# RWKV attention and two MoE stages on one core: converted weight words written over their raw tile, the converter's scratch in PSUM for two instructions longer, and another place for the rounding of the last block

## The chip, the cores and the metric

The kernel runs on one core of one Trainium2 chip. The metric is the device time of the whole program in microseconds. TensorE (PE) multiplies, with its weight loads shown apart (PEld); VectorE is DVE, ScalarE is ACT, GpSimd is POOL, and SyncE (SP) issues the transfers.

## The reference

Three stages follow one another. Only matrix products and elementwise steps over 3072 tokens matter here.

```python
# attention: 4 batches, 8 heads, 768 steps, head size 48
cur = einsum('bhd,bhe->bhde', u * k_t, v_t)
y_t = einsum('bhd,bhde->bhe', r_t, state + cur)
state = w_t[..., None] * state + einsum('bhd,bhe->bhde', k_t, v_t)
x = y.transpose(0, 2, 1, 3).reshape(3072, 384)
# first MoE: w_in (384 x 2048), w_out (2048 x 384)
h = x @ w_in
x = (h - tanh(h)) @ w_out
# second MoE: w_in2 (384 x 1024), w_out2 (1024 x 384)
h = x @ w_in2
solu = h * softmax(h)
ln = (solu - mean) / sqrt(var + 1e-6) * g_ln
out = ln @ w_out2
```

The weights arrive as 64-bit floats. A product is made of three matmuls on pairs of a rounded value and its remainder ("hi" and "lo"), so every weight and every activation is needed in these two parts.

## The kernel before, in words

**Order of the work.** The tokens are six blocks of 512 (i = 0 to 5). In the first MoE a block takes 16 steps, one for each 128 columns of w_in (m = 0 to 15), so there are 96 steps. `part1` of a step makes hp, nine matmuls into one of two PSUM banks (L334), and from it the activation; `part2` follows two steps later with nine matmuls into the three banks x2p (L357). The attention of 24 chunks of 128 tokens is spread between the steps of blocks 0 to 4, four chunks ahead of the loop. After the steps the second MoE works on 24 token tiles (b_h L412, norm, b_t L446, b_o L457). The code is written in this order, and a scheduler then settles the order of instructions on each engine by an estimate of its own; each engine runs its list in order.

**The activation in `part1`.** ACT squares hp into t (L339), DVE makes y = hp·t (L340), ACT makes the polynomial's other factor p (L342), DVE makes y = (p + c)·y (L344), ACT writes a range check over q (L345) whose only use is a sum for a flag. In block 0 p overwrites hp in PSUM and ACT rounds y into gs[0] (L347); in the other blocks p is written to the tile q in SBUF, where the check then overwrites it, and POOL rounds y (L349). POOL always makes the remainder gs[1] = y − gs[0] (L350). t, q and y have two buffers each, gs three.

**The converter, `convert` (L113 to L131).** It turns a raw tile of 128 x 768 word pairs into float values and splits them. ACT scales the low words in place (L118). For each of two halves of 384, DVE shifts and masks the high words into a scratch `a` (L125) and joins the sign and top bits (L126); the result stands in cv_x, a tile of its own in SBUF with two buffers. One DVE add over all 768 words brings in the low words (L127, shown as an operation on 1536 16-bit halves). ACT scales one half where asked (L129) and makes hi (L130); POOL makes lo (L131). `conv_a` does this for the 16 weight tiles wa of the first MoE, ahead of and during block 0, with `a` in a bank of the three-bank PSUM pool that attention uses (tile cv_a). `conv_b` does it for the eight tiles wb of the second MoE, one every second step from the first step of block 5 on (`LAST`), with `a` in cv_x itself. wb takes the place of buffers that attention frees, so it can't be written before block 5. Raw tiles have two buffers; in blocks 1 to 4 they are loaded again for a check of the weights (`check_pair`, ACT).

Of the kernel before, what the change touches and what calls it, by code (L numbers as in the profile page):

```python
# [8 lines left out]
F32 = mybir.dt.float32  # L9
F32R = mybir.dt.float32r  # L10
U32 = mybir.dt.uint32
# [3 lines left out]
ALU = mybir.AluOpType  # L15
# [4 lines left out]
NT, DM, FF, FF2 = 3072, 384, 2048, 1024  # L20
# [3 lines left out]
BLK = 512  # L24
UB = BLK // C
NB = NT // BLK
# [29 lines left out]
class Kern:  # L56
# [52 lines left out]
    def convert(self, pool, raw, hi, lo, scale=None, bank=None):  # L109

        nc, v = self.nc, self.nc.vector  # L113
        flat = raw.rearrange("p i f two -> p (i f) two")
        H_, L_ = flat[:, :, 1], flat[:, :, 0]
        x = pool.tile([128, 2 * DM], U32, tag="cv_x", name="cv_x")
        xf = x.bitcast(F32)
        nc.scalar.activation(L_, L_, AF.Copy, scale=2.0**-29)  # L118
        for i in range(2):
            s = slice(i * DM, (i + 1) * DM)  # L120
            if bank is None:
                a = x[:, s]
            else:
                a = bank.tile([128, 4, C], F32, tag="a", name="cv_a").rearrange("p j t -> p (j t)")[:, 0:DM].bitcast(U32)
            v.tensor_scalar(a, H_[:, s], 3, 0x3FFFFFF8, ALU.logical_shift_left, ALU.bitwise_and)  # L125
            v.scalar_tensor_tensor(x[:, s], H_[:, s], 0xC0000000, a, ALU.bitwise_and, ALU.bitwise_or)  # L126
        v.tensor_tensor(x, x, L_, ALU.add)  # L127
        if scale is not None:
            nc.scalar.activation(xf[:, DM:], xf[:, DM:], AF.Copy, scale=scale)  # L129
        nc.scalar.copy(hi, xf)  # L130
        nc.gpsimd.tensor_tensor(lo, xf, hi, ALU.subtract)  # L131
# [196 lines left out]
    def part1(self, i, m):  # L328
        nc, v, g = self.nc, self.nc.vector, self.nc.gpsimd
        hp = self.ps_h.tile([128, BLK], F32, tag="h", name="hp")  # L330
        xs = self.xs[i % 2]
        seq = [(a, b, j) for j in range(KM) for a, b in ((1, 0), (0, 1), (0, 0))]
        for n, (a, b, j) in enumerate(seq):
            self.mm(hp, self.wa[:, a, m, j * 128:(j + 1) * 128], xs[:, b, j], start=n == 0, stop=n == len(seq) - 1)  # L334
        t = self.gp.tile([128, BLK], F32, tag="t", name="t")
        q = self.gp.tile([128, BLK], F32, tag="q", name="q")
        y = self.gp.tile([128, BLK], F32, tag="y", name="y")
        gs = self.gs.tile([128, 2, BLK], F32R, tag="g", name="g")
        nc.scalar.activation(t, hp, AF.Square)  # L339
        v.tensor_tensor(y, hp, t, ALU.mult)  # L340
        p = hp if i == 0 else q
        nc.scalar.activation(p, t, AF.Square, bias=self.c_fsb, scale=F_S)  # L342
        col = 2 * NU + i * NM + m
        v.scalar_tensor_tensor(y, p, F_E, y, ALU.add, ALU.mult)  # L344
        self.last_act = nc.scalar.activation(q, t, AF.Relu, bias=self.c_t2, accum_out=self.flags[:, col:col + 1])  # L345
        if i == 0:
            nc.scalar.copy(gs[:, 0], y)  # L347
        else:
            g.tensor_scalar(gs[:, 0], y, 1.0, 1.0, ALU.mult, ALU.mult)  # L349
        g.tensor_tensor(gs[:, 1], y, gs[:, 0], ALU.subtract)  # L350
        return gs
# [121 lines left out]
@with_exitstack  # L473
def rwkv_moe_moe_kernel(ctx: ExitStack, tc: tile.TileContext, *args):
    nc = tc.nc
    K = Kern(tc, args)
    const = ctx.enter_context(tc.tile_pool(name="const", bufs=1))
    dram = ctx.enter_context(tc.tile_pool(name="dram", bufs=1, space=bass.MemoryType.DRAM))
    K.x2d = dram.tile([DM, NT], F32, name="x2d")
    safe = fast_path(tc, K, const)  # L480
    ok = nc.values_load(safe, min_val=0, max_val=1)
    with tc.If(ok < 1):
        general_path(tc, K, const)


def fast_path(tc, K, const):
    nc = tc.nc

    def pool(stack, name, bufs=1, side=None, **kw):
        return stack.enter_context(tc.tile_pool(name=name, bufs=bufs, side=side, reuse_waits="tile", **kw))  # L490

    K.load_act_set()
    K.setup(const)
    K.gl = const.tile([128, NM2], F32, name="gl")
    L, R, R2 = ExitStack(), ExitStack(), ExitStack()
    cv = pool(L, "cv", 2)
    cvr = pool(L, "cvr", 2)
    K.gp = pool(L, "gp", 2)
    K.gs = pool(L, "gs", 3)
    wp = pool(L, "wp")  # L500
    xp1 = pool(L, "xp1")
    xp0 = pool(R, "xp0", side="right")
    att = pool(R, "att", side="right")
    ps_x = pool(L, "ps_x", space=PSUM)
    K.ps_h = pool(L, "ps_h", 2, space=PSUM)
    K.ps_a = pool(R, "ps_a", 3, side="right", space=PSUM)
    K.wa = wp.tile([128, 2, NM, 2 * DM], F32R, name="wa")
    K.x2p = [ps_x.tile([128, BLK], F32, name=f"x2p{d}") for d in range(KM)]
    K.att_setup(att, xp0, xp1)
    K.setup_mask(K.kh[0])  # L510

    raw, gs = {}, {}
    OFF = -18
    LAST = (NB - 1) * NM
    nc.sync.dma_start(out=K.ub, in_=K.u.rearrange("h d -> (h d)").partition_broadcast(128))
    nc.scalar.activation(K.ub, K.ub, AF.Copy, scale=-1.0)
    K.att_load(0)
    K.att_load(1)
    nc.sync.dma_start(out=K.gl, in_=K.g_ln.rearrange("(k p) -> p k", p=128))

    early = 2
    SK = 2.1
    first = [(k + SK * u, K.att_pre if k < 0 else getattr(K, f"att_{k}"), u) for u in range(UB) for k in range(-1, 5)]
    first += [(SK * (u - 2) + 1.05, K.att_load, u) for u in range(2, UB + 2)] + [(SK * UB - 1, K.att_pre, UB)]
    first += [(2.0 * m, lambda m: K.conv_a(cv, cvr, m), m) for m in range(early)]
    for _, f, n in sorted(first, key=lambda e: e[0]):
        f(n)
    for s in range(-2, NB * NM + 2):
        if 0 <= s < NB * NM:
            gs[s] = K.part1(*divmod(s, NM))  # L530
        for k in (4, 0, 1, 2, 3):
            u, rem = divmod(s - OFF - k, 4)
            if rem == 0 and UB <= u < NU:
                getattr(K, f"att_{k}")(u)
        u, rem = divmod(s - OFF + 1, 4)
        if rem == 0 and UB < u < NU:
            K.att_pre(u)
        u, rem = divmod(s - OFF + 6, 4)
        if rem == 0 and UB + 1 < u < NU:
            K.att_load(u)  # L540
        if 0 <= s - 2 < NB * NM:
            K.part2(*divmod(s - 2, NM), gs.pop(s - 2))
        if 0 <= s < NM - early:
            K.conv_a(cv, cvr, s + early)
        if s == LAST:
            R.close()
            wb = pool(R2, "wb", side="right")
            K.bx = pool(R2, "bx", 2, side="right")
            K.wb = wb.tile([128, 2, NM2, 2 * DM], F32R, name="wb")
            ps_r = pool(R2, "ps_r", side="right", space=PSUM)  # L550
        if 0 <= s - LAST < NM and (s - LAST) % 2 == 0:
            K.conv_b(cv, cvr, (s - LAST) // 2)
        n, due = divmod(3 * (s - NM), 7)
        if 0 <= n < NM + NM2 and due < 3:
            K.check_pair(cvr, n)
    safe = K.safe_flag(const)
    L.close()

    K.bp = pool(L, "bp", 2)
    K.bs = pool(L, "bs", 4)  # L560
    ps_l = pool(L, "ps_l", space=PSUM)
    K.ps_t = pool(L, "ps_t", 2, space=PSUM)
    K.ps_b = (ps_r, ps_l)
    hs, ts = {}, {}
    for n in range(NTT + 2):
        if n < NTT:
            hs[n] = K.b_h(K.load_x2(n), n)
        if 0 <= n - 1 < NTT:
            ts[n - 1] = K.b_t(hs[n - 1][0])
        if 0 <= n - 2 < NTT:  # L570
            K.b_o(n - 2, ts.pop(n - 2), hs.pop(n - 2)[1])
    L.close()
    R2.close()
    return safe
# [196 lines left out]
```

## Time and profile before

| what | value |
|---|---|
| median of three runs | 837.1 us (836.93 to 837.52) |
| the profiled execution's own time | 833.47 us |
| its span | 831.7 us |
| PE busy | 779.4 us (94%) |
| DVE busy | 548.6 us (66%) |
| ACT busy | 490.5 us (59%) |
| POOL busy | 377.2 us (45%) |
| mean granted TensorE clock | 0.979 |

The shares are averages over stages that differ. Block 0 runs from about 77 to 177 us of the span, blocks 1 to 4 up to 513, block 5 to 597, and the second MoE from there.

### The profile page before, as it was taken

Reading aid. Unit: us, or ns where it says so; the run is one execution under the profiler, and the core shown is the slowest. Engines: PE = TensorE matmul, PEld = TensorE weight load, DVE = VectorE, ACT = ScalarE, POOL = GpSimd, SP = SyncE. Lnnn points to the kernel's source line nnn. Section 1 sums busy time; section 2 is a strip of 40 time slices with the busy share of each in tenths; the row PEclk is TensorE's granted clock in tenths of the full one; section 3 lists DMA queues with packets and bytes.
Section 4 is the critical chain, followed back from the end, with each engine's and each line's share of the span. In section 5 each row is a group of like instructions: output and inputs, shape, how many; then the busy total and the mean of one; then the engine's idle time right before and its main releaser. Section 6 shows DMA issues by size and latency. Waiting matters only on the chain.

```text
span 831.7 us, 13450 instructions
## 1 busy us (share of the span) xinstructions
PE 779.4 (94%) x4706; PEld 649.1 (78%) x4706; DVE 548.6 (66%) x997; ACT 490.5 (59%) x928; POOL 377.2 (45%) x360
## 2 busy tenths in 40 slices
PE   3778988999999999999999999889989999999996
PEld 2656766778878888888888788667879999999996
DVE  4688889666664566565556763895287577667763
ACT  3436776677666767677677765655445454445442
POOL 3544765655555655556556465676412111111110
PEclk9988998899999999999999999999999999999998
DMA  9966567435455554463434220410021111111101
GB/s 164 166 107 127 138 146 151 136 100 115 90 120 114 125 108 105 107 157 81 119 100 130 82 81 25 140 50 2 10 67 39 48 39 48 39 48 39 48 29 33
DMA packets 151309, 74.32 MB, mean 89 GB/s; under 512 B 107328, under 2 KB 142784, under 8 KB 151232
## 3 DMA queue, kind: packets, MB, share of 16 engines
q1 hardware_dynamic: 151232, 73.37, 37.0%
q8 instruction: 39, 0.64, 0.3%
q14 instruction: 38, 0.31, 0.1%
HBM read 61.54 MB, written 9.44 MB: 85 GB/s over the span
## 4 chain that ended last, share of the span: by engine, by line
PE 75%; DVE 11%; DMA 4%; issue 2%; POOL 2%; ACT 2%; SPq 2%; DVEq 0%; ACTq 0%; POOLq 0%
PE hp L334 19%; PE x2p L357 18%; PE o L457 12%; PE h L412 11%; PE qk L254 3%; PE tp L218 3%; DVE cv_x L126 2%; PE tt L446 2%; DVE cv_x L127 2%; PE y L296 2%; PE y L293 2%; DMA raw<-in_moe_w_out_dram 1%; DVE cv_x L125 1%; DMA raw<-in_moe_w_in_dram 1%; PE kt L260 1%
## 5 line engine op out<-in xcount | busy, mean ns | idle before, releaser
L357 PE MATMUL x2p<-g,wa 128*128 128x512 f32 x864 | 226.4, 401 | 9.0 <-POOL g L350 4.6
L334 PE MATMUL hp<-xs,wa 128*128 128x512 f32 x864 | 225.8, 403 | 6.7 <-POOL wa L131 3.2
L334 PEld LDWEIGHTS hp<-xs,wa 128*128 128x128 f32 x864 | 162.5, 192 | 45.2 <-POOL wa L131 3.7
L357 PEld LDWEIGHTS x2p<-g,wa 128*128 128x128 f32 x864 | 160.3, 191 | 46.0 <-POOL g L350 6.3
L350 POOL TENSOR_TENSOR g<-y,g 128x512 fp32r<-128x512 f32 x96 | 129.3, 1347 | 17.4 <-ACT g L347 9.7
L340 DVE TENSOR_TENSOR y<-hp,t 128x512 f32<-128x512 f32 x96 | 66.2, 689 | 106.6 <-ACT t L339 103.6
L457 PE MATMUL o<-wb,ts 128*128 128x384 f32 x576 | 110.0, 341 | 1.0 <-DVE ts L448 1.0
L345 ACT ACTIVATE q<-t,cst 128x512 f32<-128x512 f32 x96 | 69.5, 724 | 68.1 <-DVE y L344 67.8
L412 PE MATMUL h<-wb,x2s 128*128 128x512 f32 x432 | 103.8, 392 | 2.8 <-DVE so L432 2.4
L349 POOL TENSOR_SCALAR g<-y 128x512 fp32r<-128x512 f32 x80 | 53.9, 674 | 114.8 <-DVE y L344 111.4
L457 PEld LDWEIGHTS o<-wb,ts 128*128 128x128 f32 x576 | 100.5, 188 | 2.9 <-DVE ts L448 1.3
L412 PEld LDWEIGHTS h<-wb,x2s 128*128 128x128 f32 x432 | 80.6, 188 | 19.8 <-issue 3.0
L339 ACT ACTIVATE t<-hp 128x512 f32<-128x512 f32 x96 | 56.6, 591 | 44.8 <-PE hp L334 44.6
L437 POOL TENSOR_TENSOR st<-st,cst 128x1 f32<-128x1 f32 x24 | 13.5, 563 | 136.2 <-DVE st L436 134.8
L344 DVE SCALAR_TENSOR_TENSOR y<-q,y 128x512 f32<-128x512 f32 x80 | 65.4, 818 | 10.6 <-ACT q L342 5.6
L342 ACT ACTIVATE q<-t,cst 128x512 f32<-128x512 f32 x80 | 57.7, 722 | 2.0
L435 ACT ACTIVATE e<-so 128x1024 f32<-128x1024 f32 x24 | 25.4, 1059 | 49.4 <-DVE so L434 49.4
L425 DVE TENSOR_REDUCE st<-h 128x1 f32<-128x1024 f32 x24 | 29.4, 1224 | 28.6 <-PE h L412 27.1
L428 DVE TENSOR_REDUCE part<-e 128x32 f32<-128x1024 f32 x24 | 29.3, 1220 | 27.9 <-ACT e L427 27.9
L218 PE MATMUL tp<-ident,rkw 128*128 128x128 f32 x264 | 41.9, 292 | 6.0 <-DMA rkw<-in_w_dram 5.7
L402 POOL TENSOR_TENSOR x2s<-x2s 128x384 fp32r<-128x384 f32 x24 | 24.4, 1018 | 48.3 <-ACT x2s L401 40.0
L131 POOL TENSOR_TENSOR wa<-cv_x,wa 128x768 fp32r<-128x768 f32 x16 | 29.4, 1838 | 35.3 <-ACT wa L130 35.3
(114 smaller groups left out, 1211.1 us busy)
## 6 DMA issues: line engine op xcount, KB each, us to landing
raw<-in_moe_w_out_dram SPq DMA_DIRECT2D x48, 384.0 KB, 4.0
raw<-in_moe_w_in_dram SPq DMA_DIRECT2D x64, 144.0 KB, 3.2
raw<-in_moe_w_in_dram SPq DMA_DIRECT2D x16, 384.0 KB, 3.1
rkw<-in_w_dram SPq DMA_DIRECT2D x24, 192.0 KB, 4.3
rkw<-in_r_dram SPq DMA_DIRECT2D x24, 192.0 KB, 4.5
rkw<-in_k_dram SPq DMA_DIRECT2D x24, 192.0 KB, 3.9
vt<-in_v_dram SPq DMA_DIRECT2D x24, 192.0 KB, 4.4
x2d<-x2o SPq DMA_DIRECT2D x18, 256.0 KB, 2.2
```

The lines of the kernel that those rows point to most:

```text
L218: self.nc.tensor.transpose(p[:, j], self.rkw[u % 2][:, i, 2 * j:2 * j + 2, :], self.ident)
L334: self.mm(hp, self.wa[:, a, m, j * 128:(j + 1) * 128], xs[:, b, j], start=n == 0, stop=n == len(seq) - 1)
L339: nc.scalar.activation(t, hp, AF.Square)
L340: v.tensor_tensor(y, hp, t, ALU.mult)
L342: nc.scalar.activation(p, t, AF.Square, bias=self.c_fsb, scale=F_S)
L344: v.scalar_tensor_tensor(y, p, F_E, y, ALU.add, ALU.mult)
L345: self.last_act = nc.scalar.activation(q, t, AF.Relu, bias=self.c_t2, accum_out=self.flags[:, col:col + 1])
L349: g.tensor_scalar(gs[:, 0], y, 1.0, 1.0, ALU.mult, ALU.mult)
L350: g.tensor_tensor(gs[:, 1], y, gs[:, 0], ALU.subtract)
L357: self.mm(self.x2p[d], self.wa[:, a, m, sl], gs[:, b], start=m == 0 and n == 0, stop=m == NM - 1 and n == 2)
L412: self.mm(p[:, f], xs[:, a, j], self.wb[:, b, 4 * f:4 * f + 4, j * 128:(j + 1) * 128], start=q == 0, stop=q == 8)
L457: self.mm(p, ts[:, a, k], self.wb[:, b, k, DM:], start=q == 0, stop=q == 3 * NM2 - 1)
```

## The change

There are three edits. In `convert` the finished words go back over the high words of the raw tile, two words apart, and cv_x is gone; there are three raw tiles instead of two. The scratch `a` now holds the joined words too, so L126 reads and writes it, and the add is two instructions of 384 words, each from `a` and raw into raw. In `conv_a` `a` is the PSUM bank as before, used up to the add; in `conv_b` it is a tile from the ring q that `part1` also uses. Third, in block 5 p overwrites hp and ACT rounds y, as in block 0.

```diff
@@ convert
-        x = pool.tile([128, 2 * DM], U32, tag="cv_x", name="cv_x")
+        x = H_
         xf = x.bitcast(F32)
         nc.scalar.activation(L_, L_, AF.Copy, scale=2.0**-29)
         for i in range(2):
             s = slice(i * DM, (i + 1) * DM)
             if bank is None:
-                a = x[:, s]
+                a = pool.tile([128, BLK], F32, tag="q", name="cv_a")[:, 0:DM].bitcast(U32)
             else:
                 a = bank.tile([128, 4, C], F32, tag="a", name="cv_a").rearrange("p j t -> p (j t)")[:, 0:DM].bitcast(U32)
             v.tensor_scalar(a, H_[:, s], 3, 0x3FFFFFF8, ALU.logical_shift_left, ALU.bitwise_and)
-            v.scalar_tensor_tensor(x[:, s], H_[:, s], 0xC0000000, a, ALU.bitwise_and, ALU.bitwise_or)
-        v.tensor_tensor(x, x, L_, ALU.add)
+            v.scalar_tensor_tensor(a, H_[:, s], 0xC0000000, a, ALU.bitwise_and, ALU.bitwise_or)
+            v.tensor_tensor(x[:, s], a, L_[:, s], ALU.add)
@@ part1
-        p = hp if i == 0 else q
+        ends = i in (0, NB - 1)
+        p = hp if ends else q
...
-        if i == 0:
+        if ends:
             nc.scalar.copy(gs[:, 0], y)
         else:
             g.tensor_scalar(gs[:, 0], y, 1.0, 1.0, ALU.mult, ALU.mult)
@@ fast_path
-    cv = pool(L, "cv", 2)
-    cvr = pool(L, "cvr", 2)
+    cvr = pool(L, "cvr", 3)
...
-            K.conv_b(cv, cvr, (s - LAST) // 2)
+            K.conv_b(K.gp, cvr, (s - LAST) // 2)
```

The scheduler moves instructions as well. From L342 to the end of `fast_path` a line's number is one higher after the change (L344 becomes L345, L350 becomes L351).

The first place is DVE in block 5, in the middle of the conversions of `conv_b`. Before, twelve rows there read:

```order
L125 TENSOR_SCALAR cv_x<-raw 128x384 x2
L126 SCALAR_TENSOR_TENSOR cv_x<-raw,cv_x 128x384 x2
L340 TENSOR_TENSOR y<-hp,t 128x512
L127 ISA cv_x<-raw,cv_x 128x1536
L125 TENSOR_SCALAR cv_x<-raw 128x384 x2
L344 SCALAR_TENSOR_TENSOR y<-q,y 128x512
L340 TENSOR_TENSOR y<-hp,t 128x512
L126 SCALAR_TENSOR_TENSOR cv_x<-raw,cv_x 128x384 x2
L344 SCALAR_TENSOR_TENSOR y<-q,y 128x512
L127 ISA cv_x<-raw,cv_x 128x1536
L125 TENSOR_SCALAR cv_x<-raw 128x384 x2
L126 SCALAR_TENSOR_TENSOR cv_x<-raw,cv_x 128x384 x2
```

After, near the end of the block, they read:

```order
L340 TENSOR_TENSOR y<-hp,t 128x512
L125 TENSOR_SCALAR cv_a<-raw 128x384 x2
L126 SCALAR_TENSOR_TENSOR cv_a<-raw,cv_a 128x384 x2
L345 SCALAR_TENSOR_TENSOR y<-hp,y 128x512
L127 ISA raw<-raw,cv_a 128x384x2 x2
L340 TENSOR_TENSOR y<-hp,t 128x512
L345 SCALAR_TENSOR_TENSOR y<-hp,y 128x512
L340 TENSOR_TENSOR y<-hp,t 128x512
L125 TENSOR_SCALAR cv_a<-raw 128x384
L126 SCALAR_TENSOR_TENSOR cv_a<-raw,cv_a 128x384
L125 TENSOR_SCALAR cv_a<-raw 128x384
L127 ISA raw<-raw,cv_a 128x384x2
```

Before, two of the eight conversions stood in block 4 (after 70 and 71 of the 96 L340) and six followed one another closely (after 81, 82, 82, 84, 84 and 86). Now all eight stand in block 5, after 82, 84, 85, 87, 89, 91, 93 and 95, one in about two steps, with L340 and L345 between their parts.

The second place is POOL in block 5. Before, the rows with the conversions read (L402 is a remainder of the second MoE's first two tiles):

```order
L402 TENSOR_TENSOR x2s<-x2s 128x384 x2
L349 TENSOR_SCALAR g<-y 128x512
L350 TENSOR_TENSOR g<-y,g 128x512
L131 TENSOR_TENSOR wb<-cv_x,wb 128x768 x2
L349 TENSOR_SCALAR g<-y 128x512
L131 TENSOR_TENSOR wb<-cv_x,wb 128x768
L350 TENSOR_TENSOR g<-y,g 128x512
L349 TENSOR_SCALAR g<-y 128x512
L350 TENSOR_TENSOR g<-y,g 128x512
L131 TENSOR_TENSOR wb<-cv_x,wb 128x768
L349 TENSOR_SCALAR g<-y 128x512 x2
L350 TENSOR_TENSOR g<-y,g 128x512 x2
```

After, the end of the block reads:

```order
L131 TENSOR_TENSOR wb<-raw,wb 128x768
L351 TENSOR_TENSOR g<-y,g 128x512 x2
L131 TENSOR_TENSOR wb<-raw,wb 128x768
L351 TENSOR_TENSOR g<-y,g 128x512 x2
L131 TENSOR_TENSOR wb<-raw,wb 128x768
L351 TENSOR_TENSOR g<-y,g 128x512
L403 TENSOR_TENSOR x2s<-x2s 128x384 x2
```

The rounding is gone from POOL there, and its eight L131 stand two remainders apart; the last one stands ahead of the last remainder of the block. The places of `conv_a` are as before but for a position here and there.

## Rows read from the trace of the kernel before

**Rows 1.** The page's head.

```profile
span 831.7 us, 13450 instructions
```

**Rows 2.** Busy time by stage: block 0, part of block 1, block 5; columns as headed.

```profile
core 0: us, PE busy (x) PEld busy (x) DVE busy (x) ACT busy (x) POOL busy (x), PEclk, DMA share, GB/s
77.00:177.00 100.00, 91.56 (x505) 71.05 (x506) 81.37 (x141) 71.39 (x137) 62.63 (x44) 0.93 0.57 135
177.00:278.00 101.00, 101.00 (x680) 82.42 (x679) 63.85 (x111) 71.64 (x145) 56.49 (x56) 1.00 0.51 118
513.00:597.00 84.00, 77.03 (x320) 60.08 (x319) 55.61 (x64) 48.64 (x90) 51.17 (x43) 0.98 0.14 49
```

**Rows 3.** The same columns for shorter stretches of block 0 and block 5.

```profile
80.00:100.00 20.00, 19.07 (x113) 14.60 (x114) 18.50 (x32) 15.47 (x30) 13.69 (x10) 1.00 0.50 117
...
533.00:553.00 20.00, 18.27 (x77) 13.69 (x76) 18.82 (x21) 14.51 (x27) 12.71 (x10) 1.00 0.38 131
553.00:573.00 20.00, 15.99 (x60) 11.92 (x59) 15.36 (x16) 11.20 (x21) 14.33 (x12) 0.91 0.01 2
573.00:597.00 24.00, 24.00 (x107) 19.88 (x106) 9.00 (x13) 12.74 (x25) 11.45 (x12) 1.00 0.00 1
```

**Rows 4.** The chain of waits, a piece of block 5: start, us, what.

```profile
574.32 2.04 PE x2p L357 x9
```

**Rows 5.** Timeline of block 5: start, us, engine, line, operation, idle before and its releaser.

```profile
528.29 2.78 DVE L126 SCALAR_TENSOR_TENSOR cv_x<-raw,cv_x 128x384 uint32<-128x384 uint32 x2
...
528.51 2.14 POOL L131 TENSOR_TENSOR wb<-cv_x,wb 128x768 fp32r<-128x768 f32 x1
...
530.61 1.58 POOL L350 TENSOR_TENSOR g<-y,g 128x512 fp32r<-128x512 f32 x1
...
530.99 1.75 DVE L344 SCALAR_TENSOR_TENSOR y<-q,y 128x512 f32<-128x512 f32 x1
...
557.66 5.27 PE L357 MATMUL x2p<-g,wa 128*128 128x512 f32 x15 [3.19 <-POOL g L350]
```

**Rows 6.** Single DVE lines: ns minimum/median/maximum, first and last start.

```profile
L344 DVE SCALAR_TENSOR_TENSOR y<-q,y x80: 677/693/1752, 177.0 to 596.3; 128x512 f32<-128x512 f32 x80
...
L344 DVE SCALAR_TENSOR_TENSOR y<-hp,y x16: 673/682/692, 77.3 to 169.8; 128x512 f32<-128x512 f32 x16
...
L126 DVE SCALAR_TENSOR_TENSOR cv_x<-raw,cv_a x32: 532/544/557, 16.5 to 157.6; 128x384 uint32<-128x384 uint32 x32
...
L125 DVE TENSOR_SCALAR cv_x<-raw x16: 347/599/2006, 463.4 to 556.4; 128x384 uint32<-128x384 uint32 x16
...
L127 DVE CUSTOM_DVE_ANT_0 cv_x<-raw,cv_x x24: 941/954/2389, 19.1 to 561.6; 128x1536 uint16<-128x1536 uint16 x24
```

**Rows 7.** DVE in block 5, 513 to 597: busy us, mean ns, idle before and its releasers.

```profile
L344 DVE SCALAR_TENSOR_TENSOR y<-q,y 128x512 f32<-128x512 f32 x17 | 15.0, 883 | 1.8 <-ACT q L342 0.6
L126 DVE SCALAR_TENSOR_TENSOR cv_x<-raw,cv_x 128x384 uint32<-128x384 uint32 x12 | 13.2, 1136 | 0.0
...
L125 DVE TENSOR_SCALAR cv_x<-raw 128x384 uint32<-128x384 uint32 x12 | 10.5, 912 | 4.0 <-POOL wb L131 4.0
L127 DVE CUSTOM_DVE_ANT_0 cv_x<-raw,cv_x 128x1536 uint16<-128x1536 uint16 x6 | 7.1, 1190 | 0.4
```

**Rows 8.** Tile cv_x alone in block 4: span, busy on DVE, ACT, POOL.

```profile
455.00:513.00 58.00, 6.81 (x10) 1.23 (x2) 0.00 (x0) 1.00 0.21 67
```

**Rows 9.** The add L127 alone, start to end of block 0: DVE busy.

```profile
0.00:177.00 177.00, 19.16 (x16) 0.92 0.67 137
```

**Rows 10.** Lines of ACT and POOL, whole span, columns as in rows 7.

```profile
L118 ACT ACTIVATE raw<-raw 128x768 uint32<-128x768 uint32 x24 | 21.8, 910 | 17.9 <-DMA raw<-in_moe_w_out_dram 16.6 <-issue 1.2
...
L347 ACT CAST g<-y 128x512 fp32r<-128x512 f32 x16 | 9.8, 615 | 2.5 <-DVE y L344 2.4
...
L131 POOL TENSOR_TENSOR wb<-cv_x,wb 128x768 fp32r<-128x768 f32 x8 | 15.7, 1972 | 5.7 <-DVE y L344 3.4 <-ACT wb L130 2.3
```

**Rows 11.** The page's part 2: busy share of the DMA engines, 40 slices.

```profile
DMA  9966567435455554463434220410021111111101
```

More of the change, by code (lines that the diff above doesn't have):

```diff
@@ L524, in fast_path @@
     first += [(SK * (u - 2) + 1.05, K.att_load, u) for u in range(2, UB + 2)] + [(SK * UB - 1, K.att_pre, UB)]
-    first += [(2.0 * m, lambda m: K.conv_a(cv, cvr, m), m) for m in range(early)]
+    first += [(2.0 * m, lambda m: K.conv_a(K.gp, cvr, m), m) for m in range(early)]
     for _, f, n in sorted(first, key=lambda e: e[0]):
@@ L543, in fast_path @@
         if 0 <= s < NM - early:
-            K.conv_a(cv, cvr, s + early)
+            K.conv_a(K.gp, cvr, s + early)
         if s == LAST:
```

## The prediction

> **What bounds the kernel now.** I first read the page's head (a span of 831.7 us [rows 1]) and then the busy time by stage, because the 94% of PE is a mean over stages. In block 1 PE is busy all the time [rows 2], and blocks 1 to 4 and the second MoE look alike; an edit to DVE, ACT or POOL gains nothing there. Two stages are different. In block 0 PE has 8.4 of 100 us idle at a granted clock of 0.93, while DVE is busy for 81.37. Block 5 takes 84.0 us for its 320 matmuls. The chain of waits shows what they need without a wait: nine take 2.04 us [rows 4], 0.2267 us each, so 320 take 72.5 us. Thus 84.0 − 72.5 = 11.5 us are lost in block 5.
>
> Shorter stretches show where [rows 3]. From 573 on PE is busy for 24.00 of 24 us. Before that, in 533 to 553, PE runs 77 matmuls instead of the 88 that fit, with DVE busy for 18.82 of 20 us; in 553 to 573 it runs 60, and the granted clock falls to 0.91 after PE had stood still for up to 3.19 us for gs from POOL [rows 5]. So block 5 is set by the path hp, DVE, POOL, gs while six conversions lie in it.
>
> The timeline shows why DVE is full there. Two L126 at 528.29 take 2.78 us while POOL's L131 starts at 528.51 and takes 2.14; an L344 at 530.99 takes 1.75 while L350 starts at 530.61 and takes 1.58 [rows 5]. Alone, L126 takes 0.544 and L344 0.693, by their medians [rows 6]. The L344 that read p from PSUM never took over 0.692 in sixteen. An instruction of DVE with both operands in SBUF is thus held up while POOL works. [...]
>
> **Block 5, DVE's work.** By the group table [rows 7], conversions cost 10.5 + 13.2 + 7.1 = 30.8 us for six. Undisturbed they would cost 6 × (2 × 0.347 + 2 × 0.544 + 0.954) = 16.4 [rows 6], so 14.4 us, 2.4 for each, is time held up. L344 costs 15.0 against 17 × 0.682 = 11.6.
> - p in hp: L344 costs what it does in block 0, −3.4 us. The check (L345) no longer waits for L344, since p isn't in q. In return hp stays occupied until L344 is through, as in block 0.
> - The two conversions that stood in block 4, where PE hid them, now lie in block 5: +6.81 [rows 8].
> - The add in two halves: I take half of 0.954 for work that is bound by words and 0.544 for an instruction like L126, of the same shape; the second, so 8 × (2 × 0.544 − 0.954) = +1.1.
> - What the conversions are held up by stays: POOL loses L349 but gains nothing that would take L350 and L131 away. I leave the 14.4 in.
>
> Sum for DVE: 55.61 − 3.4 + 6.81 + 1.1 = 60.1 us. In block 0, which has the same form (p in hp, rounding on ACT, conversions between), DVE reached a share of 0.814 [rows 2]: 60.1/0.814 = 73.9 us.
>
> **Block 5, ACT's work.** Sixteen roundings at 0.615, 9.8 us; from the two moved conversions 1.23 for L129 [rows 8] and 0.91 for one more L118 [rows 10]. 48.64 + 9.8 + 1.23 + 0.91 = 60.6 us. Block 0 as a whole reached an ACT share of 0.714, but its best stretch 15.47/20 = 0.774 [rows 3]; by the first it is 84.9 us, by the second 78.3. I take the second, because block 0's waits include attention and transfers that block 5 doesn't have, and between 73.9 and 78.3 the middle, **76.1 us**.
>
> **The end of block 5.** The eighth L131 now stands ahead of the last L350 on POOL, by the order. Before, four remainders came after the last L131. If POOL has no slack there, PE waits for all of it: 1.97 us [rows 10]. I take it all, between 0 and 1.97, since L131 can't start before ACT's L130 of that conversion, which is late too. Block 5: 76.1 + 2.0 = 78.1, so **−5.9 us**.
>
> **The front.** Here DVE is the nearest to a bound. Sixteen adds cost 19.16 us [rows 9]; as 32 of 384 words with one operand in PSUM they cost 32 × 0.544 = 17.4, −1.8, if they cost what L126 with `a` in PSUM does. The bounds are half of 0.954 each, 15.3 (−3.9), and a full 0.954 each, 30.5 (+11.4), if the operand in PSUM halves the speed. The Trainium skill speaks for that second bound (page "VectorE: DVE Perf Modes", section "The perf-mode tier table": a two-operand instruction on 16-bit values in SBUF goes at twice the basic speed, one with any operand in PSUM at the basic speed); by it the sum would end above before, at 842.6 us, and by the row I take at 831.2. The trace has no such add; L126 is nearest, with one operand of each memory, no slower mode visible, and the same 384 words. Each `a` bank is held longer by one add, about 0.5 us, of the three that attention shares; and raw is held until POOL's L131, which cv_x was before. Against that stands a third raw tile: ACT waits 16.6 us for raw [rows 10], but the DMA engines are 0.9 and more busy in the first slices [rows 11], so earlier issue brings little. I set the front at **0**: the 1.8 against the longer bank. Its ends are −3.9 and +11.4.
>
> **Hidden parts.** L131 now reads two words apart. POOL has 38% free in block 0 and by L349's 11.1 us more in block 5 than before, so some 10% on 1.97 us is covered. In blocks 1 to 4 raw tiles are only loaded for the check, with PE busy throughout.
>
> **The sum.** The profiled execution took 833.47 us (831.7 of span and 1.8 around it), 3.6 less than the median; I take the difference over. 833.5 − 5.9 = 827.6, and on the median 837.1 − 5.9 = **831.2 us**. A difference under 0.2%, 1.7 us, can't be told from none.
>
> **The rivals.**
> - *PE becomes the bound again in block 5.* If the conversions, now one in two steps, meet POOL less often, DVE needs 60.1 − 14.4 = 45.7 and has slack. Then 72.5 + 2.0 = 74.5, −9.5, and with the front's −1.8 it is 825.8 us. For: the spread and the lighter POOL. Against: block 0, spread too, never got there. Chance 0.20.
> - *The ring of q and ACT set the pace: no gain.* In `conv_b` each half takes a q tile, and so does each check; there are two. A half can't start until an earlier check is done, and the next check not until the half's add is done. ACT has 60.6/8 = 7.6 us of work in a round of two steps; it gains nothing from 10.3 on ((84.0 − 2.0)/8), that is, if ACT waits 2.7 us in each round, about the 2.4 by which a conversion is held up. Then 837.1; at 3.2 us of waiting it is 841. The ACT share of all of block 0 (84.9 + 2.0, +2.9, 840.0) points here too. Against: DVE does both sides of this ring early in its order. Chance 0.20.
> - *The add with an operand in PSUM runs at half speed: slower.* +11.4 in the front, −5.9 in block 5: 842.6 us. It decides from 0.78 us for an add on ((19.16 + 5.9)/32). Against: L126. Chance 0.13.
>
> The forecast has 0.47.
>
> **How the numbers follow.** Its own range is 827 to 835 (front −3.9, or block 5 at 73.9 with nothing at its end; above, ACT's 78.3 and a front at +1.8). The range is 824 to 840: from the first rival with the front's best end to the second's upper price, leaving the third and the rest of the tails out. Faster by over 0.2%: forecast 0.44, first rival 0.20, second 0.05, together 0.69. Within: 0.12, most of it the second. Slower: the third's 0.13 and 0.06 of the second, 0.19.
>
> **What would show it.** The adds of `conv_a` near 0.54 us each and none near 0.95. No L345 of DVE above 0.70 us in block 5, while L125 and L126 still reach 1 us and more there. 85 or more matmuls in most 20 us of block 5, against 77 and 60, and about 78 us for its 320. On ACT, idle time before the check, ended by DVE, would speak for the second rival; 88 matmuls everywhere for the first. An idle PE at the end of block 5, ended by POOL's L351, checks the 2.0. I am wrong if an add with a PSUM operand costs over 0.78, or if hp, held longer, keeps the next part 1 waiting while a conversion stands ahead of L345 on DVE.

## The result and the profile after

The changed kernel takes 824.66 us (median of four runs, 824.2 to 826.11) against 837.31 of the kernel before (836.93 to 837.66): a ratio of 0.9852, 95% interval 0.9835 to 0.9869, or 12.4 us less by the ratio. In a second timing of both it is 0.9894 (0.9873 to 0.9915), or 8.8 us. The forecast was 5.9. The direction was right, and 824.66 lies at the low end of the range; the size was less than half of the first measurement.

The page of the changed kernel says in its head (answer to [rows 1]):

```profile
span 822.5 us, 13476 instructions
```

The spans are 9.2 us apart. To see where that is, I cut each span at four events that the timeline of every kernel shows: the first L340 (y from hp and t, whatever its line number there), the 17th (block 1's first), the 81st (block 5's first) and the last matmul of part 2. Each cut is at the event's start, rounded up to a tenth. The prediction's block 5 ran from 513 to 597; by these events it runs from 525.1 to 603.0. All times in us:

| kernel | ahead | block 0 | blocks 1 to 4 | block 5 | behind | span |
|---|---|---|---|---|---|---|
| before | 73.8 | 102.0 | 349.4 | 77.8 | 228.7 | 831.7 |
| after | 75.4 | 93.5 | 349.4 | 76.1 | 228.1 | 822.5 |
| before, second profile | 73.1 | 107.3 | 349.6 | 77.8 | 228.0 | 835.8 |
| after, second profile | 74.6 | 94.0 | 349.5 | 76.7 | 228.6 | 823.3 |

Of the 9.2 us, block 0 gave 8.5 and block 5 gave 1.7; 1.6 were lost ahead of block 0. The cuts don't hold quite the same work, though: nine matmuls of part 1 and one of part 2 that lay in block 0 before lie behind its end after, 2.3 us at 0.2267 each, and block 5 has six more of part 2, 1.4 us. By this estimate block 0 gave about 6 and block 5 about 3. The first profile of the kernel before was a quick one: its block 0 varies between executions, 102.0 and 107.3, that of the changed kernel much less. This can account for the medians of the first timing lying further apart than the first two profiles.

The busy time by stage of the kernel before, cut at these events (columns as in [rows 2]):

```profile
73.80:175.80 102.00, 91.96 (x509) 71.16 (x506) 82.58 (x145) 73.36 (x140) 64.90 (x45) 0.93 0.59 139
525.10:603.00 77.90, 70.93 (x294) 54.67 (x292) 51.56 (x61) 44.06 (x82) 44.95 (x39) 0.98 0.16 54
```

And of the changed kernel, with part of block 1 and 20 us of block 5 behind (answers to [rows 2, 3]):

```profile
75.40:168.80 93.40, 87.49 (x503) 67.78 (x500) 78.91 (x158) 71.56 (x137) 60.03 (x43) 0.98 0.66 148
518.30:594.40 76.10, 70.79 (x300) 54.47 (x298) 48.61 (x82) 55.44 (x105) 36.66 (x24) 1.00 0.19 65
170.00:271.00 101.00, 101.00 (x686) 82.99 (x683) 59.43 (x109) 70.70 (x145) 60.20 (x58) 1.00 0.50 119
...
533.00:553.00 20.00, 19.52 (x83) 15.04 (x82) 13.21 (x21) 15.71 (x30) 9.99 (x7) 1.00 0.24 79
553.00:573.00 20.00, 18.81 (x80) 14.43 (x79) 12.11 (x21) 14.03 (x27) 9.94 (x7) 1.00 0.23 79
```

In block 0 PE's idle time falls from 10.0 to 5.9 us and its busy time from 92.0 to 87.5, with ten matmuls fewer and a granted clock of 0.98 instead of 0.93. Block 1 is as full as before. In block 5 PE still has 5.3 of 76.1 us idle, and it runs 83 and 80 matmuls in two stretches of 20 us, where the prediction wanted 85 or more.

The single DVE lines of the changed kernel (answer to [rows 6]; L345 is the old L344):

```profile
L345 DVE SCALAR_TENSOR_TENSOR y<-hp,y x32: 666/688/693, 77.4 to 589.2; 128x512 f32<-128x512 f32 x32
...
L127 DVE CUSTOM_DVE_ANT_0 raw<-raw,cv_a x48: 541/549/565, 18.6 to 585.7; 128x768 uint16<-128x768 uint16 x48
```

An add of 384 words with an operand in PSUM takes 0.549 us, and none over 0.565, where a whole one of 768 took up to 2.389. In block 0 the whole adds of the kernel before took 1.255 on average:

```profile
L127 DVE CUSTOM_DVE_ANT_0 cv_x<-raw,cv_x 128x1536 uint16<-128x1536 uint16 x13 | 16.3, 1255 | 0.1
```

DVE in block 5 (answer to [rows 7], from 518.3 to 594.4):

```profile
L126 DVE SCALAR_TENSOR_TENSOR cv_a<-raw,cv_a 128x384 uint32<-128x384 uint32 x16 | 12.5, 807 | 0.1
L340 DVE TENSOR_TENSOR y<-hp,t 128x512 f32<-128x512 f32 x16 | 11.0, 687 | 15.0 <-ACT t L339 15.0
L345 DVE SCALAR_TENSOR_TENSOR y<-hp,y 128x512 f32<-128x512 f32 x16 | 11.0, 685 | 10.7 <-ACT hp L343 10.7
L125 DVE TENSOR_SCALAR cv_a<-raw 128x384 uint32<-128x384 uint32 x16 | 9.0, 585 | 2.5 <-DMA x2d<-x2o 2.5
L127 DVE CUSTOM_DVE_ANT_0 raw<-raw,cv_a 128x768 uint16<-128x768 uint16 x16 | 8.5, 548 | 0.1
```

Eight conversions cost 12.5 + 9.0 + 8.5 = 30.0 us of DVE there, as much as six did before (30.8). DVE is no longer full, and now waits for ACT.

Why the add was worth so much shows in the chain of waits. Before, in block 0:

```profile
99.48 2.08 DVE cv_x L127
...
103.39 4.16 DMA raw<-in_moe_w_out_dram
...
113.97 1.72 DVE cv_x L127
...
117.52 3.38 DMA raw<-in_moe_w_out_dram
```

The add's end frees one of two raw tiles; only then is the next load issued. Issuing takes 1.8 us and the load 3.4 to 4.2, so the next conversion can go on 5 to 6 us after the add's end. By this chain an add that POOL holds up for a microsecond delays the whole loop. After the change the same chain runs through more engines, because raw is freed by POOL:

```profile
125.35 0.57 DVE raw L127
...
125.94 0.90 ACT wa L130
...
126.91 1.89 POOL wa L131
...
130.60 3.35 DMA raw<-in_moe_w_out_dram
```

The clock in block 0 differs too. Before, the stretch from 128.0 to 141.2 and the two behind it read:

```profile
128.00:141.20 13.20, 10.29 (x62) 7.82 (x61) 12.78 (x22) 8.84 (x17) 10.48 (x7) 1.00 0.77 150
141.20:151.40 10.20, 10.20 (x31) 7.89 (x30) 7.65 (x14) 6.65 (x13) 6.47 (x5) 0.50 0.77 203
151.40:161.00 9.60, 9.60 (x77) 7.56 (x76) 8.01 (x15) 6.13 (x10) 4.20 (x3) 1.00 0.29 90
```

PE was busy for 10.29 of 13.2 us while DVE was busy for 12.78; then the granted clock is 0.50 for 10.2 us (1.2 instead of 2.4 GHz), and PE, busy throughout, gets through 31 matmuls (the 77 behind them are in good part short ones of attention). In all, block 0 had 13.7 us at the lower level before and 3.4 after. Ahead of block 0 it is the other way round in these two profiles, 13.7 us before and 44.4 after, which is why the mean granted clock of the whole span is lower after the change, 0.969 against 0.979. In the second profile of the changed kernel it is 13.7 there as well, and the stretch ahead is again 1.5 us longer than before. So the 1.6 us lost there aren't put down to the clock; their cause stays open.

### The profile page after: what moved, and what is told of

It is laid out like the page before. It is cut to its first block, busy times and chain, and to the rows that moved or that the text cites. A ratio compares the mean times of both kernels' runs of the same rounds, so it can differ in the third digit from the quotient of the medians.

```text
span 822.5 us, 13476 instructions
## 1 busy us (share of the span) xinstructions
PE 776.5 (94%) x4706; PEld 647.6 (79%) x4706; DVE 528.3 (64%) x1021; ACT 498.8 (61%) x944; POOL 365.3 (44%) x344
## 4 chain that ended last, share of the span: by engine, by line
PE 71%; ACT 4%; issue 3%; DVE 2%; DMA 2%; POOL 1%; SPq 1%; ACTq 0%; POOLq 0%; DVEq 0%
PE hp L334 17%; PE x2p L358 17%; PE o L458 12%; PE h L413 11%; PE tp L218 3%; PE tt L447 2%; PE qk L254 2%; PE y L296 2%; PE y L293 2%; DMA raw<-in_moe_w_out_dram 1%; PE kt L260 1%; PE ds L270 1%; DVE cv_a L125 1%; ACT q L346 1%; ACT wb L130 0%
## 5 line engine op out<-in xcount | busy, mean ns | idle before, releaser
L358 PE MATMUL x2p<-g,wa 128*128 128x512 f32 x864 | 223.4, 397 | 4.8 <-ACT g L348 3.7
L358 PEld LDWEIGHTS x2p<-g,wa 128*128 128x128 f32 x864 | 158.5, 188 | 40.7 <-ACT g L348 5.2
L351 POOL TENSOR_TENSOR g<-y,g 128x512 fp32r<-128x512 f32 x96 | 126.6, 1318 | 39.9 <-ACT g L348 22.2
L340 DVE TENSOR_TENSOR y<-hp,t 128x512 f32<-128x512 f32 x96 | 66.2, 690 | 103.3 <-ACT t L339 96.7
L346 ACT ACTIVATE q<-t,cst 128x512 f32<-128x512 f32 x96 | 69.5, 724 | 60.7 <-DVE y L345 59.3
L350 POOL TENSOR_SCALAR g<-y 128x512 fp32r<-128x512 f32 x64 | 44.1, 689 | 84.0 <-DVE y L345 76.6
L345 DVE SCALAR_TENSOR_TENSOR y<-q,y 128x512 f32<-128x512 f32 x64 | 52.1, 814 | 8.2 <-ACT q L343 4.4
L343 ACT ACTIVATE q<-t,cst 128x512 f32<-128x512 f32 x64 | 46.3, 723 | 1.8
L245 POOL TENSOR_SCALAR_AFFINE_SELECT aq<-dg 128x1024 f32<-128x1024 f32 x24 | 27.7, 1155 | 43.9 <-PE y L296 33.7
L428 ACT ACTIVATE e<-h,st 128x1024 f32<-128x1024 f32 x24 | 26.8, 1115 | 32.7 <-DVE st L427 31.9
```

Source lines behind the costliest of these rows:

```text
L358: self.mm(self.x2p[d], self.wa[:, a, m, sl], gs[:, b], start=m == 0 and n == 0, stop=m == NM - 1 and n == 2)
```

## The experiments

Each was timed against the kernel before on the same chip. A stage is cut as in the table above. All measured stages are collected behind the last of them.

**Two raw tiles instead of three.** The changed kernel with

```diff
-    cvr = pool(L, "cvr", 3)
+    cvr = pool(L, "cvr", 2)
```

Expected: 

> The changed kernel with two raw tiles instead of three. The traces put the gain in block 0: from its first L340 to that of block 1 it takes 93.5 us instead of 102.0, and 75.3 instead of 73.7 are spent ahead of it. Theory A (the add, now with one operand in PSUM, is no longer held up by POOL: 0.55 us for each half, against 1.26 on average for a whole before): the third tile matters little, 824.7 to 827 us. Theory B (the third raw tile: weights arrive earlier, so the loop of load, convert, free no longer sets block 0): a raw tile is now held until POOL has made lo, with two of them the loop is longer than before, and block 0 gives back its 7 us and more, 831 to 838 us.

Measured: 830.89 us, ratio 0.9952 (0.9934 to 0.9969); block 0 takes 104.1 us. In the form in which raw is held until POOL is through, the third tile is worth 104.1 − 93.5 = 10.6 us of block 0, of which 2.4 come back ahead of it and 1.1 in blocks 1 to 4, so 7.0 of the span. Theory A expected at most 827; 830.89 lies just under theory B's 831 to 838; but this alone doesn't say that the third tile beats the kernel before, which had two and cv_x.

**Without the third edit.** The changed kernel with

```diff
-        ends = i in (0, NB - 1)
+        ends = i == 0
```

Expected: 

> The changed kernel without its third edit: in block 5 p goes to q and POOL rounds, as before. The front should stay as in the changed kernel. By the prediction's term block 5 gives back 5.9 us: 830.6. By the traces, where block 5 (first L340 to the last matmul of part 2) went from 77.8 to 76.1 us and took over the two conversions that stood in block 4, it gives back 2 to 4 us: 827 to 829. If block 5's gain comes from the spread conversions and the adds and not from this edit: 825 to 826.

Measured: 833.17 us, 0.9968 (0.9953 to 0.9983). Block 5 takes 83.1 us, 5.3 more than before the change, so the third edit is worth 7.0 us beside the other two: more than each theory gave it. DVE in block 5 of this kernel:

```profile
L125 DVE TENSOR_SCALAR cv_a<-raw 128x384 uint32<-128x384 uint32 x16 | 17.3, 1084 | 0.2 <-DMA x2d<-x2o 0.2
L345 DVE SCALAR_TENSOR_TENSOR y<-q,y 128x512 f32<-128x512 f32 x16 | 14.2, 889 | 1.4 <-ACT q L343 0.6 <-ACT raw L129 0.5
L126 DVE SCALAR_TENSOR_TENSOR cv_a<-raw,cv_a 128x384 uint32<-128x384 uint32 x16 | 12.6, 789 | 0.3
L127 DVE CUSTOM_DVE_ANT_0 raw<-raw,cv_a 128x768 uint16<-128x768 uint16 x16 | 12.0, 751 | 0.5
```

Without the third edit the shift L125 takes 1.084 us on average, with it 0.585; the add 0.751 and 0.548. The three lines cost 41.9 us here and 30.0 in the changed kernel.

**The third edit alone.** The kernel before with p in hp and ACT's rounding in block 5.

```diff
-        p = hp if i == 0 else q
+        p = hp if i in (0, NB - 1) else q
...
-        if i == 0:
+        if i in (0, NB - 1):
```

Expected: 

> The kernel before with the third edit alone: in block 5 p goes to hp and ACT rounds. By the prediction's term for block 5, 5.9 us less than before: 831.4. If that edit is worth what the traces show for block 5, 2 to 4 us less: 833 to 835. If ACT and the longer held hp take the gain away while the adds still stand with both operands in SBUF: within 1 us of before. L344 in block 5 should in no case take over 0.70 us.

Measured: 832.99 us, 0.9981 (0.9965 to 0.9996). Block 5 falls from 77.8 to 76.4 us. Of the 5.9 us forecast for block 5 this edit by itself brings 1.4; the run ahead of this one shows it worth five times as much where all eight conversions lie in block 5 with their scratch in SBUF.

**The add alone.** The kernel before, with two raw tiles and cv_x, and in the converter of the first MoE:

```diff
-            v.scalar_tensor_tensor(x[:, s], H_[:, s], 0xC0000000, a, ALU.bitwise_and, ALU.bitwise_or)
-        v.tensor_tensor(x, x, L_, ALU.add)
+            if bank is None:
+                v.scalar_tensor_tensor(x[:, s], H_[:, s], 0xC0000000, a, ALU.bitwise_and, ALU.bitwise_or)
+            else:
+                v.scalar_tensor_tensor(a, H_[:, s], 0xC0000000, a, ALU.bitwise_and, ALU.bitwise_or)
+                v.tensor_tensor(x[:, s], a, L_[:, s], ALU.add)
+        if bank is None:
+            v.tensor_tensor(x, x, L_, ALU.add)
```

Expected: 

> The kernel before, with two raw tiles and cv_x, and only the add of the first MoE's conversions changed: the joined words stay in PSUM and the add is two instructions of 384 words, from PSUM and raw into cv_x. Conversions for the second MoE are as before. Theory A (the add was held up by POOL): L127 in the front takes 0.55 us for each half, and block 0 gains most of the 7 us: 829 to 832. Theory B (the third raw tile): 836 to 838.

Measured: 827.77 us, 0.9916 (0.9891 to 0.9941), 7.0 us less by the ratio; block 0 takes 91.9 us, no more than in the changed kernel. Its add (L130 there) and its row for block 0:

```profile
L130 DVE CUSTOM_DVE_ANT_0 cv_x<-raw,cv_a 128x768 uint16<-128x768 uint16 x26 | 14.0, 546 | 0.4 <-ACT g L352 0.2
```

```profile
74.70:166.60 91.90, 85.35 (x527) 66.06 (x526) 80.69 (x158) 72.26 (x139) 58.80 (x43) 1.00 0.67 147
```

DVE's work is 1.9 us less than before, PE's idle time 3.5 us less (6.5 instead of 10.0), and no part of block 0 is at the lower clock. Nine matmuls of part 1 and nine of part 2 that lay in block 0 before lie in the blocks behind it here, which take 2.4 us more than before. Blocks 0 to 4 together are the fairer measure: 443.7 us against 451.4, 7.7 less, and as much as in the changed kernel's two profiles (442.9 and 443.5). Theory A holds: the front's gain is the add's. The third raw tile only pays for raw being held longer.

**The changed kernel again.** Unaltered, for a second timing and a second profile.

Expected: 

> The changed kernel unaltered, beside the other runs of this call. The first timing had it 12.6 us below before, the two profiled executions are only 9.2 us apart. If the stages of the profile tell the whole, the ratio comes out at 0.986 to 0.990 here; if the first timing holds, at 0.985 or below. Block 0 (first L340 to block 1's) again 92 to 95 us, block 5 (first L340 to the last matmul of part 2) 75.5 to 77.

Measured: 825.97 us, 0.9894 (0.9873 to 0.9915). The gain differs between the two timings, 12.4 and 8.8 us; the kernel before is 2.3 us quicker in the second, 834.98. Why is open. The second rests on more executions, 17 and 6 instead of four each, and those of the kernel before range from 832.4 to 838.5 us; the four of the first all lie at 836.9 and above.

**The cut without PSUM.** The kernel before with two adds of 384 words in the converter of the first MoE, both operands in SBUF:

```diff
-        v.tensor_tensor(x, x, L_, ALU.add)
+        if bank is None:
+            v.tensor_tensor(x, x, L_, ALU.add)
+        else:
+            for i in range(2):
+                s = slice(i * DM, (i + 1) * DM)
+                v.tensor_tensor(x[:, s], x[:, s], L_[:, s], ALU.add)
```

Expected: 

> The kernel before with the first MoE's add cut into two instructions of 384 words, but from cv_x and raw, both in SBUF: the cut without PSUM. If what helped is that POOL no longer holds the add up, nothing is gained: halves of 0.55 us at the least and 1 us and more when POOL works, block 0 at 100 to 104 us, 834 to 838 us in all. If what helped is the cut, so that other DVE work gets in between, block 0 falls to 95 us or less: 830 or less.

Measured: 835.83 us, 1.0011 (0.9991 to 1.0031): no change. Block 0 takes 104.3 us. Its add and its row for block 0:

```profile
L132 DVE CUSTOM_DVE_ANT_0 cv_x<-raw,cv_x x32: 542/550/2685, 18.5 to 162.0; 128x768 uint16<-128x768 uint16 x32
```

```profile
74.20:178.50 104.30, 89.16 (x529) 67.46 (x531) 86.97 (x157) 73.60 (x140) 64.20 (x45) 1.00 0.58 133
```

Undisturbed the half takes what it takes from PSUM, 0.550 by the median, but up to 2.685. It isn't the cut that helps but the operand's place. This block 0 has no stretch at the lower clock and is as long as before, with PE idle for 15.1 us, so the waiting alone is enough to make it long.

**All scratch in SBUF.** The changed kernel, with

```diff
-        self.convert(pool, raw, self.wa[:, 0, m], self.wa[:, 1, m], bank=self.ps_a)
+        self.convert(pool, raw, self.wa[:, 0, m], self.wa[:, 1, m])
```

Expected: 

> The changed kernel, but the first MoE's conversions take their scratch from the ring q in SBUF, as those of the second MoE do, instead of PSUM: three raw tiles and the halved add stay. If the operand in PSUM is what helped, shift, join and add in the front are held up again (L127 up to 1 us and more) and block 0 takes 100 us or more: 830 to 840 us. If three raw tiles and the halved add help by themselves: 825 to 828.

Measured: 854.75 us, 1.0241 (1.0215 to 1.0266), well beyond both expectations. Block 0 takes 133.4 us. DVE's costliest lines there:

```profile
L125 DVE TENSOR_SCALAR cv_a<-raw 128x384 uint32<-128x384 uint32 x28 | 22.5, 818 | 0.1
L127 DVE CUSTOM_DVE_ANT_0 raw<-raw,cv_a 128x768 uint16<-128x768 uint16 x28 | 22.0, 797 | 0.1
```

The hold-up is back, and 27.3 us are at the lower clock; but the conversions also share the ring q with part 1, and this run can't part the two. L126 there, with both operands in SBUF, takes 0.548 us on average and isn't held up; why it is the shift ahead of it and the add behind it that wait isn't shown. Some 8.5 us come back in blocks 1 to 4, because more of the attention's matmuls lie in block 0 here (686 matmuls in all, 503 in the changed kernel).

**Block 5's scratch in PSUM.** The changed kernel, with the scratch of the second MoE's conversions in a bank that a later product of that MoE uses:

```diff
-                a = pool.tile([128, BLK], F32, tag="q", name="cv_a")[:, 0:DM].bitcast(U32)
+                a = pool.tile([128, DM], F32, tag="o", name="cv_a").bitcast(U32)
...
-            K.conv_b(K.gp, cvr, (s - LAST) // 2)
+            K.conv_b(ps_r, cvr, (s - LAST) // 2)
```

Expected: 

> The changed kernel with the scratch of the second MoE's conversions in a PSUM bank that is free in block 5, instead of the ring q. If the ring and what is left of POOL's hold on shift and join cost time there, L125, L126 and L127 stay at 0.55 us, and block 5 falls from 76.1 us towards 73: 2 to 3 us below the changed kernel. If block 5 is by now set by PE and hp: within 1 us of it.

Measured: 821.13 us, 0.9828 (0.9805 to 0.9851). Block 5 takes 70.7 us instead of 76.1, 5.4 less, about twice what was expected. No L125, L126 or L127 in this kernel takes over 0.570 us. L125 in the changed kernel and here:

```profile
L125 DVE TENSOR_SCALAR cv_a<-raw x48: 346/555/1451, 15.6 to 582.4; 128x384 uint32<-128x384 uint32 x48
```

```profile
L125 DVE TENSOR_SCALAR cv_a<-raw x48: 536/556/568, 15.9 to 546.6; 128x384 uint32<-128x384 uint32 x48
```

The conversions also move: the last shift starts at 546.6 us instead of 582.4, and five of the 16 halves now lie ahead of block 5, where PE stays busy throughout, so that DVE has 67 instructions in block 5 instead of 82. How much of the 5.4 us is the ring q, how much the hold-up and how much the earlier place, this run can't part.

**Both in PSUM, with cv_x and two raw tiles.** The kernel of the add alone with the third edit, and with both converters' scratch in PSUM.

Expected: 

> The kernel before with two raw tiles and cv_x, and these edits: both converters join and add with the scratch in PSUM (a free bank in block 5), the halves go to cv_x, and block 5 has p in hp and ACT's rounding. If the stages add up: 74.7 us ahead, 91.9 for block 0 as in the run with the split add, 350 for blocks 1 to 4, 70.7 for block 5 as in the run with the second scratch in PSUM, 228.4 behind, a span of 816 us and about 817.5 in all, 0.979 of before. If the third raw tile is needed beside the cut add: 821 or more.

Measured: 819.04 us, 0.9808 (0.9783 to 0.9832); the stages come out within 1.2 us of those expected, and block 0 doesn't need the third raw tile beside this add.

**Block 5's scratch in PSUM, without the third edit.**

Expected: 

> The run with the second scratch in PSUM, without the third edit (p in q, POOL rounds in block 5). In the changed kernel that edit was worth 83.0 - 76.1 = 6.9 us of block 5. If it is worth that because POOL's rounding holds the conversions up, and these no longer read two operands from SBUF, block 5 stays within 1.5 us of 70.7 and the whole within 0.2% of 821. If it is worth it by itself, through L345 and POOL's load: block 5 74 us or more, 825 or more.

Measured: 817.05 us, 0.9789 (0.9766 to 0.9812), the quickest of all. Block 5 takes 67.5 us. Its row for block 5, and L345's there:

```profile
518.80:586.30 67.50, 67.50 (x299) 55.30 (x297) 43.61 (x67) 46.43 (x86) 45.10 (x40) 1.00 0.21 71
```

```profile
L345 DVE SCALAR_TENSOR_TENSOR y<-q,y 128x512 f32<-128x512 f32 x16 | 16.3, 1025 | 1.6 <-ACT q L343 0.9
```

PE has no idle time left. L345 with p in q is held up to 1.025 us on average, and it costs nothing here: DVE is busy for only 43.61 of 67.5 us and PE throughout. The conversions lie where they do in the run with the third edit (eleven halves in block 5 in both). So once they are out of POOL's way, the third edit costs 70.7 − 67.5 = 3.2 us: block 5 lies below both expectations, and the one that the edit would then be worth nothing was too kind to it.

**Half of the third edit.** The changed kernel with p in hp, but POOL's rounding in block 5:

```diff
-        if ends:
+        if i == 0:
```

Expected: 

> The changed kernel with only half of its third edit: in block 5 p goes to hp, but POOL rounds. Block 5 is 76 us with both halves and 83 with none. If POOL's rounding is what holds shift, join and add up, it stays at 81 to 83 and L125 at about 1.1 us on average: 830 to 833 us. If L345's two operands in SBUF are, it falls to 78 or less: 826 to 828.

Measured: 828.51 us, 0.9921 (0.9895 to 0.9947). Block 5 takes 78.6 us, between the two expectations: of the third edit's 7.0 us, p in hp gives 4.5 and ACT's rounding 2.5. L125 takes 0.763 us on average there, and the three lines of the conversions cost 35.6 us: of the 11.9 us by which the third edit shortens them, 5.6 are the rounding's and 6.3 those of p in hp.

**The kernel before again**, for a second profile.

Expected: 

> The kernel before unaltered, for a second profile of it. Block 0 (first L340 to block 1's) 100 to 104 us, block 5 (first L340 to the last matmul of part 2) 77 to 79, and the granted clock at half for 10 us or more of block 0, if the first profile is typical. If the half clock there was an accident of that execution, block 0 takes 96 to 98.

Measured: 837.64 us in one run; block 0 takes 107.3 us, more than expected, with 17.1 us of it at the lower clock. The first profile's 13.7 were no accident.

| run | ahead | block 0 | blocks 1 to 4 | block 5 | behind | span |
|---|---|---|---|---|---|---|
| two raw tiles | 73.0 | 104.1 | 348.3 | 76.2 | 227.9 | 829.5 |
| without the third edit | 74.8 | 96.3 | 349.5 | 83.1 | 228.6 | 832.3 |
| third edit alone | 73.5 | 103.0 | 349.6 | 76.4 | 228.4 | 831.0 |
| add alone | 74.7 | 91.9 | 351.8 | 77.8 | 228.7 | 824.9 |
| cut, both in SBUF | 74.2 | 104.3 | 349.3 | 77.8 | 229.0 | 834.7 |
| all scratch in SBUF | 73.6 | 133.4 | 340.9 | 76.6 | 228.1 | 852.6 |
| block 5's scratch in PSUM | 74.2 | 96.5 | 349.7 | 70.7 | 228.4 | 819.4 |
| both in PSUM, cv_x | 74.6 | 92.1 | 351.2 | 70.9 | 228.5 | 817.3 |
| the same scratch, no third edit | 75.0 | 94.2 | 349.7 | 67.5 | 228.2 | 814.5 |
| p in hp only | 75.5 | 95.2 | 349.5 | 78.6 | 229.0 | 827.7 |

Six profiles have the changed kernel's edits to the front: their block 0 takes 93.5 to 96.5 us. Differences of block 0 below 3 us are therefore not read as an effect.

## Why the prediction missed the size

**The front is the step that failed.** "I set the front at 0: the 1.8 against the longer bank" should have read 7 us less: 1.6 more ahead of block 0 and 8.5 less in it, and in the second pair of profiles 1.5 more and 13.3 less (block 0 from 107.3 to 94.0; about 2 us of either is work that moved behind the cut). The price of an add was right, 0.549 us against the 0.544 taken, and so was DVE's saving, which is 1.6 us for all 32 (17.6 against 19.16 [rows 9]). What was wrong was to take the saving in DVE's work for the saving in time. The 19.16 us hold 16 adds that take 0.954 when let alone, 15.3, and 3.9 us in which POOL held them up. I saw such a hold-up in block 5, where I looked for it, and never looked for it in block 0. There it sits on the loop of two raw tiles: an add's end starts a load, and the load the next conversion. The add alone is worth 7.7 us of blocks 0 to 4 by the profiles and 7.0 of the whole by the timing; the same cut with both operands in SBUF is worth nothing. The DMA shares that I set against a gain there, 0.9 and more [rows 11], cover only the first 42 us; in block 0 the share is 0.59, and what the loads stood on was the free raw tile.

How far the clock takes part isn't shown. Of the 10.1 us by which the add alone shortens block 0, 3.5 are idle time of PE and 6.6 are PE busy for less long; in these lie both the matmuls that moved on and the 13.7 us at the lower level that are gone. What brought the clock down stays open: the rows around 141 show it falling behind a stretch with waits, but with the cut in SBUF PE was idle for 15.1 us of block 0, more than before's 10.0, and the clock stayed up. That run was long without a fall, so none is needed for the waits to cost their time.

**Block 5 was over-sized.** −5.9 was forecast and −1.7 measured (−1.1 in the second pair). The parts behave as follows. L345 from PSUM is never over 0.693 us: right. "What the conversions are held up by stays" was wrong: L125 falls from 0.912 [rows 7] to 0.585 us and the eight conversions cost what six did, because the third edit, which I counted as no help to them, takes away much of what held them up: about half of that by the rounding and half by p in hp, as the last run but one shows (half of the third edit). DVE thereby has time to spare (48.6 of 76.1 us busy), so a share of 0.814 as in block 0 was no guide to the time. What fills the block instead is shown in part. Of PE's 5.3 us of idle time 2.4 are waits for hp, held until L345 is through, which is the prediction's own sign of being wrong:

```profile
PE hp L334 <- DVE y L345: 2.4, 2, 1.7
```

With the scratch in PSUM, and the conversions earlier for it, the block takes 70.7 us, and with p in q as well 67.5; what the ring q costs by itself wasn't parted. The conversions that came in from block 4, with their new scratch, cost 5.3 us without the third edit, and the third edit gave 7.0 back.

**The end of block 5** was set at 2.0 us and is small: the last L351 waits for ACT, not for the last L131, and only a product of the second MoE waits for that one, 0.9 us.

**The rivals.** The first gave 825.8, close to the measured time, but by a block 5 bound by PE. DVE's slack came about (48.6 us busy, 45.7 in the rival), the bound didn't; the number is right by chance. The second is neither shown nor refuted in its mechanism: moving the scratch out of the ring of q brings 5.4 us of block 5, together with the remaining hold-up and the earlier conversions. That it would take all the gain didn't come about. The third is refuted: the add with an operand in PSUM goes at full speed. With it falls what I took from the Trainium skill (page "VectorE: DVE Perf Modes", section "The perf-mode tier table"): 768 16-bit values of one source in PSUM and one in SBUF take 0.549 us, and with both in SBUF 0.550 by the median, so the place of the operand cost nothing here.

## What to carry to other kernels

Where DVE and POOL share a stage, compare each DVE line's mean with its minimum: what lies between is hold-up, and here an operand moved to PSUM removed it (adds of block 0 from 1.255 us on average to 0.546 for each half, blocks 0 to 4 from 451.4 to 443.7 us). Ask of such an instruction what its end sets free: where it was the buffer of the next load, the gain was that of the loop, 7.7 us, several times the 1.9 that DVE saved. And try a cure for one hold-up again without its companion: here the third edit gave 7.0 us beside a scratch in SBUF and cost 3.2 beside one in PSUM.

## What the runs showed of the hardware that was not expected

It is not only instructions with both operands in SBUF that POOL holds up. A shift from SBUF to SBUF (L125), with one operand, takes 0.35 us at the least, 0.585 on average beside POOL's remainders, 0.763 with POOL's roundings added and 1.084 with p in q besides; [rows 6] had it at up to 2.006. From SBUF to PSUM it takes 0.55 and in no run over 0.573. So the quicker form by itself was the slower one in company. And the granted clock fell in block 0 of the kernel before in both of its profiles (13.7 and 17.1 us), and not at all in four of the others, among them the cut with both operands in SBUF, whose block 0 was no shorter and had more idle time of PE.
